# Global keys folded into the next-tile score blocks, and the first batch reordered, in a fused attention and phase-mixing kernel

## The chip, the cores and the metric

The kernel runs on one core of a Trainium2 chip. The metric is the device time of one execution in microseconds (us). A "median" is the median of several executions; the "span" is the length of one profiled execution from its first to its last instruction and is about 2 us shorter than its time. Engines are named as in the profile: PE is TensorE (PEld its weight loads), DVE is VectorE, ACT is ScalarE, POOL is GpSimd, SP is SyncE; "PEclk" is the TensorE clock that was granted, as a share of full speed.

## The reference

There are two stages. The first is attention with 4 batches, 8 heads, 768 positions and 64 columns per head. A query sees the keys 0 to 95 positions behind it and the first 8 keys ("global" keys), whatever their distance:

```python
rel = pos[:, None] - pos[None, :]
is_global = pos[None, :] < 8
is_local = (rel >= 0) & (rel < 96)
dist = np.where(is_global & ~is_local, 96.0, np.abs(rel))
scores = scale * q @ k.T - slope[h] * dist       # where is_global | is_local, else -1e9
x = softmax(scores) @ v                          # heads side by side: (4, 768, 512)
```

The second stage takes x, per batch:

```python
theta = x @ w_theta                              # (768, 512)
y = w_tok_r @ (x * cos(theta)) + w_tok_i @ (x * sin(theta))
u = x + y
out = u + relu(u @ w_ch)
```

## The kernel before

A sequence is 6 tiles of 128. Scores are built transposed, keys on the partitions. A tile of 128 keys is seen by 224 queries: its own 128, and the first 96 of the next tile. The exponentials are multiplied with a table `etab` that holds the exponential of the distance bias, and zeros where nothing is to be seen. Two heads form a pair; a 64-row matmul of each runs in one half of the array.

```python
def globals_(b):                                   # the 8 global keys, all queries, once per batch
    for hh in range(2):
        pg = ps_big()...
        for p in range(NP):                        # 4 pairs, 32 rows of the output each
            for c0, c1 in ((0, 512), (512, S)):
                nc.tensor.matmul(pg[GS*p:GS*(p+1), c0:c1], lhsT=kT[R, 0:GS], rhs=qT[R, c0:c1], ...)
        nc.scalar.activation(e_, pg[:, 0:S], AF.Exp, scale=scale, bias=gbias[:, hh:hh+1])
        nc.vector.tensor_mul(e_[:, 0:T], e_[:, 0:T], gmask)

def scores(b, p, c):                               # two key tiles: 2 tiles x 2 heads, 224 columns
    for j in range(2):
        jt = 2 * c + j
        n = min(W, S - jt * T)                     # W = 224
        for hh in range(2):
            nc.tensor.matmul(pb[:, hh, j*W:j*W+n], lhsT=kT[R, jt*T:(jt+1)*T], rhs=qT[R, jt*T:jt*T+n], ...)
    ...                                            # exp on ACT, times etab on DVE

def vglob(b, p):                                   # v of the global keys to the pair's 32 rows
    nc.tensor.matmul(pv, lhsT=shift[:, p, :], rhs=vn[:, 2*p:2*p+2, 0, :], ...)
    nc.scalar.copy(out=vg, in_=pv)

def values(b, p, hh):                              # 17 matmuls: own tile, tile before, globals
    for it in range(NT):
        mms = [(e_t[:, hh, it, 0:T], vn[:, 2*p+hh, it, :])]
        if it:
            mms.append((e_t[:, hh, it-1, T:2*T], vn[:, 2*p+hh, it-1, :]))
        mms.append((egs[b][hh][:, it*T:(it+1)*T], vg[:, hh, :]))
        ...
```

The second stage is PE work: `theta` (x times w_theta), `mix` (the two 768 x 768 token matrices) and `chan` (u times w_ch). The attention of batch b+1 is woven between the matmuls of `mix` of batch b. Batch 0's attention has nothing to hide behind; it is a prologue in which the order on PE is fixed by hand. `theta` needs x transposed and `chan` needs u transposed. For batches 1 to 3 both are DMAs, and `chan` of a tile comes two tiles behind its `mix`:

```python
def utrans(b, tt):
    if b and (b, tt) != (B - 1, NT - 1):
        nc.sync.dma_start_transpose(out=uT, in_=u)     # SP's queue
        return
    ...                                                # else on PE, copied by ACT

def chan(b, tt):
    for dc in range(NC):
        nc.tensor.matmul(ps_c, lhsT=uT[:, dc, :], rhs=w_ch_bf[:, dc, :], ...)
```

q, k and v are loaded with a change of type by DMAs from POOL. The tile for a batch's q and k has one buffer, so the load of the next batch's q and k starts when the last pair of this one has been copied out of it.

The softmax here doesn't subtract the row's maximum and nothing guards it: scores larger than these inputs give would overflow.

## Time and profile before

The median was 193.61 us (193.41 to 193.78, 3 runs). The profiled execution took 192.08 us (span 190.0 us, clock 1.00) and is quicker than those three.

The page of the kernel before, its parts 1 (busy time and share of each engine), 2 (clock in 40 slices, in tenths) and 4 (the chain of work that ended last, by engine):

```profile
PE 174.4 (92%) x1616; PEld 89.8 (47%) x1641; DVE 131.3 (69%) x305; ACT 108.0 (57%) x162; POOL 27.0 (14%) x31
PEclk9999999999999999999999999999999999999999
PE 65%; ACT 15%; DVE 8%; DMA 6%; issue 3%; POOL 1%; ACTq 0%; SPq 0%; POOLq 0%
```

PE is the engine to relieve, but not everywhere.

What the pieces cost on PE stands in the chain of waits, in order of time (start, length, what), taken from the mix of batch 1:

```profile
91.90 0.45 PE pb L227 x8
92.34 0.32 PE ps L352
...
93.65 0.30 PE pb L249 x4
93.95 0.54 PE ps L352 x2
94.48 0.52 PE pb L298 x17
...
97.26 0.97 PE ps L377 x4
```

L227 is half of the global scores, L249 a chunk of local scores, L298 the values of a head, L352 mix and L377 chan. A mix matmul takes 0.216 us among its like, but 0.32 us before a group of 64-row matmuls. The Trainium skill (TensorEngine Tiling (Array Packing), Key Properties) says that a change of tiling mode drains TensorE; the extra 0.1 us here agrees.

### The profile page before, as it was taken

To read this page: it belongs to the slowest core of one execution; us is meant where nothing else is said; L and a number is where in the kernel's file an instruction comes from. 1 tells how busy PE (TensorE), PEld (TensorE's weight loads), DVE (VectorE), ACT (ScalarE), POOL (GpSimd) and SP (SyncE) were. 2 spreads that over 40 slices of the span, in tenths; PEclk is the share of its full clock that TensorE was granted. 3 is DMA by queue.
4 is the path that set the end of the run, shared out by engine and by line. 5 is a ranking of instruction groups with operands and counts; after the bars stand their busy time and mean duration, and the time that the engine had idled before them with its cause. 6 is when DMAs were issued, how large, how long until landed. Compare 5 with 4: busy or idle time off the path is not lost.

```text
span 190.0 us, 3965 instructions
## 1 busy us (share of the span) xinstructions
PE 174.4 (92%) x1616; PEld 89.8 (47%) x1641; DVE 131.3 (69%) x305; ACT 108.0 (57%) x162; POOL 27.0 (14%) x31
## 2 busy tenths in 40 slices
PE   7868698999999999999999999999999999999981
PEld 2434386445735565643354454543554454434430
DVE  4699696487976886996587568986667753734422
ACT  2399987842697764489963450899644704800010
POOL 7992264000030002130000000000000000000000
PEclk9999999999999999999999999999999999999999
DMA  4999999999999833999925458111145254114432
GB/s 61 162 173 158 209 210 208 204 197 146 128 182 219 124 97 100 113 161 192 207 45 120 122 123 131 56 55 31 24 104 124 54 139 141 59 29 109 138 86 110
DMA packets 58082, 23.98 MB, mean 126 GB/s; under 512 B 44240, under 2 KB 54992, under 8 KB 58064
## 3 DMA queue, kind: packets, MB, share of 16 engines
q0 software_dynamic: 35760, 12.85, 72.2%
q1 hardware_dynamic: 22304, 10.88, 23.1%
q8 instruction: 13, 0.21, 0.4%
q14 instruction: 5, 0.04, 0.1%
HBM read 25.69 MB, written 6.29 MB: 168 GB/s over the span
## 4 chain that ended last, share of the span: by engine, by line
PE 65%; ACT 15%; DVE 8%; DMA 6%; issue 3%; POOL 1%; ACTq 0%; SPq 0%; POOLq 0%
PE ps L352 27%; PE ps L377 10%; PE pb L333 9%; PE pb L298 7%; PE pb L249 5%; DMA uT<-u 3%; PE ps L207 3%; DMA qk<-in_k_dram 3%; ACT cs L337 2%; ACT kT L214 2%; ACT e_108 L253 2%; PE ps L170 2%; DVE qT L212 1%; DVE qkn L199 1%; DVE zri L341 1%
## 5 line engine op out<-in xcount | busy, mean ns | idle before, releaser
L352 PE MATMUL ps<-zri,w_tokT_119 128*128 128x512 bf16 x136 | 51.6, 381 | 1.2 <-DVE zri L341 0.5
L352 PE MATMUL ps<-zri,w_tokT_120 128*128 128x512 bf16 x138 | 52.2, 379 | 0.5 <-issue 0.2
L377 PE MATMUL ps<-w_ch_bf,uT 128*128 128x512 bf16 x89 | 23.5, 380 | 1.2 <-DMA uT<-u 0.6
L341 DVE TENSOR_TENSOR zri<-x_sb,cs 128x512 bf16<-128x512 bf16 x48 | 18.3, 422 | 9.1 <-ACT cs L337 7.7
L357 DVE TENSOR_TENSOR u<-x_sb,ps 128x512 bf16<-128x512 bf16 x24 | 16.5, 686 | 11.6 <-PE ps L352 11.1
L333 PE MATMUL pb<-w_theta_bf,xT 128*128 128x512 bf16 x93 | 23.2, 379 | 0.2
L352 PEld LDWEIGHTS <-w_tokT_119 128*128 128x128 bf16 x144 | 14.0, 97 | 17.8 <-issue 4.2
L380 DVE SCALAR_TENSOR_TENSOR o_sb<-ps,u 128x512 f32<-128x512 f32 x24 | 16.5, 686 | 7.5 <-PE ps L377 6.6
L214 ACT COPY kT<-ps 128x768 bf16<-128x768 bf16 x16 | 12.9, 806 | 12.9 <-PE ps L207 12.8
L352 PEld LDWEIGHTS <-w_tokT_120 128*128 128x128 bf16 x144 | 14.1, 98 | 12.5 <-issue 1.4
L371 ACT COPY uT<-ps 128x512 bf16<-128x512 bf16 x7 | 4.1, 587 | 27.0 <-PE ps L370 27.0
L249 PE MATMUL pb<-qT,kT 64*128 64x224 bf16 x192 | 17.2, 254 | 2.3 <-ACT e_110 L253 0.7
L337 ACT ACTIVATE cs<-pb,halfpi 128x1024 bf16<-128x1024 f32 x12 | 13.4, 1119 | 9.1 <-issue 7.2
L207 PE MATMUL ps<-ident,qkn 128*128 128x128 bf16 x192 | 15.0, 222 | 0.9 <-DVE ident L101 0.4
L207 PEld LDWEIGHTS <-qkn 128*128 128x128 bf16 x192 | 11.9, 99 | 7.8 <-DVE qkn L199 5.5
L212 DVE COPY qT<-ps 128x768 bf16<-128x768 bf16 x16 | 15.1, 948 | 0.0
L249 PEld LDWEIGHTS <-kT 64*128 64x128 bf16 x192 | 6.3, 94 | 16.1 <-issue 13.5
L78 POOL DMA_DIRECT2D vn<-in_v_dram x5 | 9.5, 1921 | 24.9 <-DVE rec L306 20.9
L333 PEld LDWEIGHTS <-xT 128*128 128x128 bf16 x96 | 8.9, 98 | 8.8 <-ACT xT L319 0.3
L377 PEld LDWEIGHTS <-uT 128*128 128x128 bf16 x96 | 8.1, 98 | 10.4 <-DMA uT<-u 2.1
L199 DVE COPY qkn<-qk 128x768 bf16<-128x768 bf16 x30 | 10.8, 387 | 3.1 <-DMA qk<-in_q_dram 3.1
L177 PE MATMUL ps<-zero 128*128 128x512 bf16 x28 | 10.4, 473 | 2.4 <-DVE zero L88 1.4
(129 smaller groups left out, 280.9 us busy)
## 6 DMA issues: line engine op xcount, KB each, us to landing
out_dram<-o_sb SPq DMA_DIRECT2D x24, 256.0 KB, 2.3
qk<-in_q_dram POOLq DMA_DIRECT2D x3, 768.0 KB, 8.6
qk<-in_k_dram POOLq DMA_DIRECT2D x3, 768.0 KB, 12.3
vn<-in_v_dram POOLq DMA_DIRECT2D x3, 768.0 KB, 23.5
w_nat<-in_moe_w_tok_r_dram POOLq DMA_DIRECT2D x3, 384.0 KB, 15.9
w_nat<-in_moe_w_tok_i_dram POOLq DMA_DIRECT2D x3, 384.0 KB, 16.8
qk<-in_q_dram POOLq DMA_DIRECT2D x4, 192.0 KB, 5.3
qk<-in_k_dram POOLq DMA_DIRECT2D x4, 192.0 KB, 5.8
```

What stands on the lines that cost most here:

```text
L207: nc.tensor.transpose(ps[:, t_, :], qkn[:, t_, i_].rearrange("p h d -> p (h d)"), ident)
L212: nc.vector.tensor_copy(out=dst, in_=src)
L214: nc.scalar.copy(out=dst, in_=src)
L249: nc.tensor.matmul(pb[:, hh, j * W:j * W + n], lhsT=kT[R, jt * T:(jt + 1) * T], rhs=qT[R, jt * T:jt * T + n], start=True, stop=True)
L298: nc.tensor.matmul(o, lhsT=l_, rhs=r_, start=(i_ == 0), stop=(i_ == len(mms) - 1))
L333: nc.tensor.matmul(pb[:, j, :], lhsT=xT[:, dc, st * T:(st + 1) * T], rhs=w_theta_bf[:, dc, :], start=(dc == 0), stop=(dc == NC - 1))
L337: nc.scalar.activation(cs[:, 0], pb, AF.Sin, bias=halfpi)
L341: nc.vector.tensor_mul(zri[b][:, i_, 2 * c + j_, :].rearrange("p (g d) -> p g d", g=NP), xb[:, :, 2 * c + j_, :], cs[:, i_, j_].rearrange( ...
L352: anchor["pe"] = nc.tensor.matmul(ps, lhsT=w_tokT[wi][:, st, tt * T:(tt + 1) * T], rhs=zri[b][:, wi, st, :], start=(st == 0 and wi == 0), ...
L357: anchor["dve"] = nc.vector.tensor_add(u_sb[b, tt].rearrange("p (g d) -> p g d", g=NP), x_sb[b][:, :, tt, :], ps.rearrange("p (g d) -> p g ...
L377: nc.tensor.matmul(ps_c, lhsT=uT[:, dc, :], rhs=w_ch_bf[:, dc, :], start=(dc == 0), stop=(dc == NC - 1))
L380: nc.vector.scalar_tensor_tensor(o_sb, in0=ps_c, scalar=0.0, in1=u, op0=ALU.max, op1=ALU.add)
```

## The change

In the second score block of a key tile (the next tile's 128 queries), only keys 33 to 127 are ever near enough: the first rows of that block are always zero. The change puts the 8 global keys into rows 0 to 7 of these blocks. For that it makes a copy `kG` of the transposed keys, and a copy `vG` of v, in which the first 8 keys of each tile are replaced by the global ones. All blocks become 128 wide, the table gets five slots of 128 (the own block of the first tile, where the global keys are seen by every later query; a next-tile block; the own block of other tiles; and the last two again, so that each chunk finds its slots in a row), and the global scores, their exponentials, the shift matmuls and 6 of the 17 value matmuls per head go away. The first batch's order is also rewritten: v is loaded before the last two pairs of q and k, and values and x transposes are interleaved with the scores instead of coming at the end.

```diff
     alloc_loads(0)
-    for p in range(NP):
-        load_qk(0, 2 * p, 2)
+    load_qk(0, 0, 2)
+    load_qk(0, 2, 2)
     load_v(0, 0, 4)
+    load_qk(0, 4, 2)
+    load_qk(0, 6, 2)
     load_v(0, 4, 4)
 ...
+        nc.vector.tensor_copy(out=kG, in_=kT[:, T:(NT - 1) * T].rearrange("p (t n) -> p t n", t=NT - 2))
+        nc.vector.tensor_copy(out=kG[:, :, 0:NG], in_=kT[:, None, 0:NG].to_broadcast([T, NT - 2, NG]))
 ...
-    def globals_(b):
-        ...
     def scores(b, p, c):
 ...
-            n = min(W, S - jt * T)
-            for hh in range(2):
-                nc.tensor.matmul(pb[:, hh, j * W:j * W + n], lhsT=kT[R, jt * T:(jt + 1) * T],
-                                 rhs=qT[R, jt * T:jt * T + n], start=True, stop=True)
+            for part in range(2 if jt + 1 < NT else 1):
+                for hh in range(2):
+                    lhsT = kG[R, jt - 1, :] if part and jt else kT[R, own]
+                    o = (2 * j + part) * T
+                    nc.tensor.matmul(pb[:, hh, o:o + T], lhsT=lhsT, rhs=qT[R, (own, nxt)[part]],
+                                     start=True, stop=True)
 ...
+    def vglob(b, h0, n):
+        with behind("dve"):
+            nc.vector.tensor_copy(out=vG[:, hs], in_=vn[:, hs, 1:NT - 1, :])
+        nc.vector.tensor_copy(out=vG[0:NG, hs], in_=vn[0:NG, hs, 0:1, :].to_broadcast([NG, n, NT - 2, D + 1]))
     def values(b, p, hh):
 ...
-                mms.append((e_t[:, hh, it - 1, T:2 * T], vn[:, 2 * p + hh, it - 1, :]))
-            mms.append((egs[b][hh][:, it * T:(it + 1) * T], vg[:, hh, :]))
+                mms.append((e_t[:, hh, it - 1, 1, :], vG[:, h, it - 2, :] if it > 1 else vn[:, h, 0, :]))
 ...                                              # the prologue of batch 0
-        for p in range(1, NP):
-            prep(0, p, 2 if p == 1 else 0)
-            ...
-            for c in range(NT // 2):
-                scores(0, p - 1, c)
-                warm(1)
-        globals_(0)
-        ...                                       # last pair's scores, all values, all x transposes
+        for p in range(1, NP + 1):
+            if p < NP:
+                prep(0, p, 2 if p == 1 else 0)
+                bias_table(p)
+            if p == 2:
+                vglob(0, 0, 4)
+            if p == 3:
+                vglob(0, 4, 4)
+            for c in range(NT // 2):
+                scores(0, p - 1, c)
+                if p == 1:
+                    warm(1)
+            if p > 1:
+                values(0, p - 2, 0)
+                values(0, p - 2, 1)
+            if p > 2:
+                xtrans(0, p - 3, nc.scalar.copy)
```

`warm(n)` is n matmuls on zeros that nothing reads; they keep PE's clock up. `behind("dve")` places a copy in the order behind the last u addition.

## The prediction

> **What bounds the kernel now.** TensorE. The page has PE busy 174.4 of 190.0 us, DVE 69%, ACT 57%; PE holds 65% of the chain that ended last; the granted clock is 1.00. By stretches: from 35.7 to 152 us PE is busy 98%. The first 35.7 us differ: from 9.5 to 23.5 us ACT is busy 14.00 of 14.00 us, PE only 10.0; the chain there runs DMA, then ACT. The last stage (165 to 190 us) has no attention. At the batch boundaries (76 to 84.3, 116 to 126 us) DVE is also full: 8.30 of 8.30 and 9.70 of 10.0.
>
> **What goes from PE, per batch** (chain and timeline views):
> - global scores: 2 groups of 8 matmuls, 0.45 us each, plus about 0.095 us each because the matmul before them takes 0.31 instead of 0.216 us: 1.1 us. The Trainium skill (TensorEngine Tiling, Key Properties) says a change of tiling mode drains the array; these gaps agree.
> - 4 shift matmuls, 0.113 us start to start: 0.45 us.
> - values: 11 matmuls instead of 17 per head; 17 take 0.52 us, so 48 x 30 ns = 1.45 us.
>
> **Added to PE:** 22 score matmuls of 128 columns per head pair instead of 12 of 224/128. The two row halves overlap: a 224 pair takes about 107 ns, a chunk 298 ns with the drain. A 128 pair should take 56 to 67 ns, a chunk about 340: about 0.1 us per head pair, 0.4 us per batch. If weight loads hold pairs to 107 ns, it is +0.45 us per head pair.
> Net about -2.55 us per batch; three batches' attention lies in the PE-bound stretch: -7.6 us.
>
> **Other engines.** ACT loses, per batch, two global exponentials (0.95 us) and four vg copies (0.28), and gains about 0.08 us per head pair; eight table exponentials grow from 0.39 to about 0.52 us. DVE gains kG copies (about 0.35 us per head pair, scaled from 0.34 us for 768 elements) and vG copies (about 1.2 us per batch at the four-element rate that the skill, VectorE: DVE Perf Modes, gives for bf16 copies in SBUF; the qkn copies agree), and loses 0.45 us of gmask work: about +2 us per batch.
>
> **What is given back.** The kG copies fall into the boundaries where DVE is full: +0.3 us each. Without the globals, the first pair's values follow its scores sooner (about 1.8 instead of 3.8 us): +0.3 us per batch. Together +1.8.
> Prologue: no globals, values interleaved; but v is loaded before the third pair, and DVE, in order, waits for v at the vG copies (landings estimated at 11.6 and 19.2 us); ACT work hardly shrinks: only -0.7 us.
>
> **Prediction:** 193.6 - 7.6 + 1.8 - 0.7 = 187.1 us, range 183.8 to 190.0. Faster 0.82, same 0.16, slower 0.02.
>
> **What would show it.** Value groups of 11 matmuls in about 0.34 us; score chunks 0.33 to 0.36 us start to start (0.47 means weight-load bound); both mix stretches (89 to 116, 126 to 152 us before) 2 to 2.5 us shorter; first theta within 1.5 us of before; last stage equal; ACT down about 10 us, DVE up about 5.
>
> **What would make it wrong.** vG copies at one element per cycle[...]; score pairs bound by weight loads; the two score buffers shared with values making PE wait for exponentials that less PE work covers; a prologue that waits for v lengthen, or that gains several us because values no longer queue at its end.

## More of the kernel before

The windows view gives busy time per engine in stretches. I cut the span at six milestones: the first sine of batch 0; the last u of batch 0; the first and last u of batch 1; the first and last u of batch 2. The stretches are then the prologue, the mix of batch 0, a boundary (theta, and preparing the next q and k), the mix of batch 1, a boundary, the mix of batch 2, and the rest. The columns are: stretch, its length, busy time and count for PE, PEld, DVE, ACT and POOL, granted clock, DMA share, GB/s.

```profile
0.00:34.08 34.08, 27.17 (x326) 15.69 (x329) 24.64 (x84) 24.97 (x45) 21.26 (x26) 1.00 1.38 169
34.08:75.89 41.81, 40.05 (x427) 22.86 (x434) 32.47 (x71) 27.09 (x40) 2.98 (x3) 1.00 1.77 155
75.89:90.12 14.23, 13.86 (x104) 7.12 (x104) 12.16 (x28) 10.95 (x13) 2.73 (x3) 1.00 1.42 154
90.12:116.17 26.05, 25.74 (x268) 12.52 (x272) 17.61 (x36) 14.09 (x24) 0.00 (x0) 1.00 0.63 116
129.82:155.98 26.16, 25.60 (x267) 12.39 (x270) 17.60 (x36) 14.09 (x24) 0.00 (x0) 1.00 0.34 81
```

In the three mix stretches PE is busy 96 to 99% of the time; in the prologue only 80% (27.17 of 34.08). A matmul removed from a mix stretch should shorten it; one removed from the prologue need not.

## The result, and the profile after

| | before | after |
|---|---|---|
| median, us | 193.51 (193.34 to 193.78, 4 runs) | 191.17 (190.57 to 191.51, 4 runs) |
| profiled execution, us | 192.08 | 191.4 |
| span, us | 190.0 | 189.6 |
| granted clock, mean | 1.00 | 0.973 |

The ratio is 0.9874, with a 95% interval of 0.9844 to 0.9905. A ratio here is the mean time of one kernel's fast runs over that of the other's fast runs of the same rounds, so it is not quite the ratio of the medians. The kernel is 1.3% faster, which at a threshold of 2% counts as the same, and the time is above the predicted range.

The page of the kernel after, the same three parts:

```profile
PE 167.9 (89%) x1500; PEld 89.1 (47%) x1523; DVE 137.9 (73%) x309; ACT 102.9 (54%) x122; POOL 27.1 (14%) x31
PEclk9999669999999999999987999999999999999999
PE 55%; ACT 14%; DVE 13%; DMA 12%; issue 2%; POOL 2%; ACTq 0%; POOLq 0%
```

PE is 6.5 us less busy, yet the span is only 0.4 us shorter. DMA has gone from 6% to 12% of the chain, and the clock has two dents, in the slices from 19 to 28 us and from 95 to 104 us. The windows view of the kernel after, cut at the same milestones:

```profile
0.00:35.49 35.49, 26.36 (x293) 16.84 (x296) 25.96 (x76) 24.82 (x35) 21.03 (x26) 0.90 1.29 175
35.49:75.38 39.89, 37.91 (x399) 21.87 (x405) 34.10 (x74) 25.51 (x30) 4.14 (x3) 1.00 1.84 146
75.38:89.33 13.95, 13.79 (x111) 7.22 (x112) 13.00 (x36) 10.88 (x13) 1.88 (x3) 1.00 1.37 144
89.33:117.83 28.50, 24.88 (x233) 12.16 (x236) 18.66 (x32) 12.45 (x14) 0.00 (x0) 0.94 0.66 124
131.51:155.64 24.13, 23.06 (x232) 11.66 (x234) 18.58 (x32) 12.45 (x14) 0.00 (x0) 1.00 0.44 86
```

Some matmul records are missing from each trace, so the counts of PE are a few per cent off. The lengths are not affected. As differences, after less before (from the milestones before they were rounded for the view, so that a last digit can differ):

| stretch | before | after | difference |
|---|---|---|---|
| prologue | 34.08 | 35.49 | +1.41 |
| mix of batch 0 | 41.81 | 39.89 | -1.92 |
| boundary | 14.23 | 13.95 | -0.28 |
| mix of batch 1 | 26.05 | 28.50 | +2.45 |
| boundary | 13.65 | 13.69 | +0.04 |
| mix of batch 2 | 26.16 | 24.12 | -2.04 |
| rest | 33.98 | 33.99 | +0.01 |

Two of the three mix stretches gained 2 us each, as intended. The mix of batch 1 does the same work as that of batch 2, took almost the same time in the kernel before, and now takes 4.38 us longer. The prologue is 1.4 us longer. These are the two questions.

**The mix of batch 1.** The chain of the kernel after, from its start:

```profile
90.08 8.61 DMA uT<-u
98.69 0.05 issue
98.74 1.89 PE ps L357 x4
...
102.49 0.33 PE pb L278 x11
102.83 0.33 PE pb L230 x8
```

L357 is chan, L278 the values of a head and L230 a score chunk. The last two lines are the intended gain: 0.33 us instead of 0.52 for values, 0.33 instead of 0.30 for a chunk. The lines above are new. The transpose of batch 1's first u tile took 8.61 us, and PE waited for it. Its four matmuls then took 1.89 us instead of 0.97, at a lowered clock (0.50 for 3.41 us, from 98.45 us on). The summary line of the transposes of u (issue to landing), for the kernel before:

```profile
DMA to landing us min/median/max: 2.4/2.4/6.0
```

and for the kernel after:

```profile
DMA to landing us min/median/max: 2.4/2.4/8.6
```

The longest is the first of batch 1 in both. Before, it was issued at 90.9 and landed at 96.9, and chan wanted it at 97.26: 0.4 us to spare, invisible in the profile. At the same time the q and k of batch 3 are being loaded. The DMA view between 80 and 100 us gives the times from issue to landing, before:

```profile
qk<-in_k_dram POOLq DMA_DIRECT2D x1, 768.0 KB, 12.3
```

and after:

```profile
qk<-in_k_dram POOLq DMA_DIRECT2D x1, 768.0 KB, 13.6
```

With the issue at 84.02 and 84.85 us (timeline of POOL), k landed at 96.3 and 98.4 us, and the transpose within 0.6 us of it in both. So the sum closes: PE was ready for chan 1.4 us sooner (its last matmul before the wait ended at 95.84, where chan began at 97.26 before), the transpose landed 1.8 us later (98.7 against 96.9), and 0.4 us were to spare; that gives the wait of 2.9 us. The Trainium skill (DMA: Bandwidth & Descriptors, Queues, rings and completion order) says that each DMA engine takes turns between queues at packet granularity, so a short transfer shares with a long one. No run here shows the turns, and sharing need not be all of it. A store of the output stands ahead of the transpose on SP's queue. In the kernel after it was issued at 86.04 us and took 7.2 us (DMA view between 80 and 100 us); in after_qk2, below, the store before the same transpose took 2.0 us:

```profile
out_dram<-o_sb SPq DMA_DIRECT2D x1, 256.0 KB, 7.2
```

It landed at 93.26 us, and the packet records of the trace have the transpose's first 256-byte packet at 93.94 us, 3.9 us after its issue (93.19 and 94.04 us in the kernel before; in after_qk2 the first packet follows the issue by 1.2 us). So the load may have delayed the transpose in part by way of the store. No run moved the store, so the shares are open.

**The prologue.** The windows view of the kernel before, in the busy part:

```profile
14.00:19.00 5.00, 4.24 (x48) 2.37 (x47) 5.00 (x13) 5.00 (x11) 1.38 (x2) 1.00 2.78 158
19.00:24.00 5.00, 3.32 (x52) 1.78 (x51) 2.87 (x7) 5.00 (x12) 1.28 (x2) 1.00 1.19 209
```

and of the kernel after:

```profile
14.00:19.00 5.00, 2.90 (x46) 2.08 (x48) 5.00 (x16) 4.59 (x7) 2.38 (x4) 1.00 1.86 183
19.00:24.00 5.00, 4.03 (x64) 3.36 (x64) 5.00 (x16) 4.80 (x8) 2.18 (x3) 0.59 1.17 209
```

Before, ACT had no gap from 9.5 us to 24 us. After, DVE is full from 14 to 24 us (5.00 of 5.00 twice), ACT is not, and in the second window PE runs at a clock of 0.59. The timeline (start, length, engine, line, what, and in brackets the idle time before it and what ended it) shows the start of it in the kernel after:

```profile
12.38 0.43 DVE L259 COPY vG<-vn 128x1040 bf16<-128x1040 bf16 x1 [3.48 <-DMA vn<-in_v_dram]
...
14.41 2.64 ACT L234 ACTIVATE e<-pb 128x1024 bf16<-128x1024 f32 x3 [1.75 <-PE pb L230]
```

where the kernel before had

```profile
12.59 1.71 ACT L253 ACTIVATE e_108<-pb 128x896 bf16<-128x896 f32 x2
```

DVE, which works in order, waited 3.48 us for v, and behind the copy of v stood the copies that the second pair's scores and the kG of the first needed. The first exponential came 1.8 us later.

One caution for all prologues below. Traces of one and the same prologue differ: the first sine came at 34.08 and 34.99 us in the kernel before and in before_qk2, and at 35.49, 35.94 and 36.49 us in the kernel after, after_qk2 and after_uTpe. So the new prologue is 0.5 to 2.4 us longer by these traces, and a difference of less than 1 us between two single traces shows nothing.

### The profile page after: what moved, and what is told of

The parts are those of the page before. It is cut to its first block, busy times and chain, and to the rows that moved or that the text cites. A ratio compares the mean times of both kernels' runs of the same rounds, so it can differ in the third digit from the quotient of the medians.

```text
span 189.6 us, 3693 instructions
## 1 busy us (share of the span) xinstructions
PE 167.9 (89%) x1500; PEld 89.1 (47%) x1523; DVE 137.9 (73%) x309; ACT 102.9 (54%) x122; POOL 27.1 (14%) x31
## 4 chain that ended last, share of the span: by engine, by line
PE 55%; ACT 14%; DVE 13%; DMA 12%; issue 2%; POOL 2%; ACTq 0%; POOLq 0%
PE ps L332 22%; PE ps L357 10%; DMA uT<-u 8%; PE pb L313 7%; ACT e L234 6%; PE pb L230 5%; DMA vn<-in_v_dram 4%; PE pb L278 4%; DVE qT L203 4%; ACT cs L317 3%; PE ps L198 3%; DVE qkn L189 2%; PE ps L278 2%; DVE zri L321 2%; POOL qk L72 2%
## 5 line engine op out<-in xcount | busy, mean ns | idle before, releaser
L234 ACT ACTIVATE e<-pb 128x1024 bf16<-128x1024 f32 (+1 forms) x48 | 44.1, 958 | 25.8 <-PE pb L230 25.7
L357 PE MATMUL ps<-w_ch_bf,uT 128*128 128x512 bf16 x94 | 25.3, 391 | 3.7 <-DMA uT<-u 3.5
L242 DVE TENSOR_TENSOR e<-e,etab 128x1024 bf16<-128x1024 bf16 (+1 forms) x32 | 19.7, 617 | 3.5 <-ACT e L234 3.5
L230 PE MATMUL pb<-qT,kT 64*128 64x128 bf16 x224 | 17.9, 231 | 4.7 <-ACT e L234 4.6
L230 PEld LDWEIGHTS <-kT 64*128 64x128 bf16 x224 | 10.0, 99 | 18.3 <-issue 16.7
L278 PEld LDWEIGHTS <-e 128*128 128x128 bf16 x352 | 14.7, 100 | 6.8 <-issue 1.0
L198 PE MATMUL ps<-ident,qkn 128*128 128x128 bf16 x192 | 16.1, 232 | 1.1 <-DVE qkn L189 0.9
L198 PEld LDWEIGHTS <-qkn 128*128 128x128 bf16 x192 | 12.8, 103 | 8.4 <-DVE qkn L189 6.1
L230 PE MATMUL pb<-qT,kG 64*128 64x128 bf16 x128 | 13.6, 228 | 2.0 <-DVE kG L210 2.0
L357 PEld LDWEIGHTS <-uT 128*128 128x128 bf16 x96 | 8.4, 99 | 13.5 <-DMA uT<-u 4.7
```

The lines of the kernel that those rows point to most:

```text
L198: nc.tensor.transpose(ps[:, t_, :], qkn[:, t_, i_].rearrange("p h d -> p (h d)"), ident)
L230: nc.tensor.matmul(pb[:, hh, o:o + T], lhsT=lhsT, rhs=qT[R, (own, nxt)[part]], start=True, stop=True)
L234: ins = nc.scalar.activation(e_c, pb[:, :, 0:n], AF.Exp, scale=scale).ins
L242: nc.vector.tensor_mul(e_c, e_c, tab[:, :, s0:s0 + n // T].rearrange("p a s n -> p a (s n)"))
L278: nc.tensor.matmul(o, lhsT=l_, rhs=r_, start=(i_ == 0), stop=(i_ == len(mms) - 1))
```

## The experiments

All kernels gave correct results. Kernels of one group ran on one chip and share the runs of the kernel before. Each edit is against the kernel after unless it says otherwise.

### Group 1: the two causes, one at a time

Theory: the lost time of batch 1 is the DMA transpose slowed by the load of q and k, and the prologue's is DVE's wait for v. Rivals: the stretch of batch 1 is slow because the new attention work itself stalls PE there; and the prologue is slow because of the cold clock.

**after_qk2** takes the load away from the transpose. With two q and k buffers it can start much earlier. To fit in memory, other buffers had to shrink; PE, ACT and DVE keep their order of work.

```diff
-        qk = ld.tile([T, 2, H, NT, D], BF, name="qk", bufs=1)
+        qk = ld.tile([T, 2, H, NT, D], BF, name="qk", bufs=2)
...                       # qT, kT, kG: bufs 6 -> 4; vG: bufs 2 -> 1
```

> The changed kernel with two buffers for the q and k loads in place of one (fewer buffers of qT, kT, kG and vG make room); the order of the compute instructions is the same, only the loads of later batches move earlier. Theory A (TensorE's saving in batch 1's mix was lost because the first two DMA transposes of u there share the DMA engines with the q/k load of batch 3, and TensorE now arrives before they land): the first transpose lands in about 2.4 us in place of 8.6, the 3 us wait near 98 us goes, the clock stays at 1.00 there, the stretch between the first and the last u of batch 1 takes about 25 us in place of 28.5, the whole kernel about 188 us. Rival B (the score buffers and the exponentials limit that stretch): the stretch stays at 28 us, the kernel at 191.

Median 187.39 us (186.91 to 188.62, 4 runs) beside 193.33 us of the kernel before (7 runs, 191.99 to 195.7, two of them slow), ratio 0.9723 (0.9655 to 0.9792). The summary line of its transposes of u, and, from its windows view, the mix of batch 1:

```profile
DMA to landing us min/median/max: 2.4/2.4/3.8
```

```profile
89.78:113.90 24.12, 23.61 (x237) 11.86 (x236) 18.58 (x31) 12.46 (x14) 0.00 (x0) 1.00 0.41 93
```

The first transpose of batch 1 took 2.45 us, the stretch took 24.12 us instead of 28.50, exactly that of batch 2, and the clock was 1.00. No other stretch moved by more than 0.5 us (prologue 35.94, first mix 39.89, boundaries 13.95 and 13.69, last mix 24.12). PE's attention work there was never the trouble.

**after_uTpe** leaves the loads alone and takes the transpose off the DMA: this one tile of u is transposed on PE and copied by ACT.

```diff
-        if b and (b, tt) != (B - 1, NT - 1):
+        if b and (b, tt) not in ((1, 0), (B - 1, NT - 1)):
             nc.sync.dma_start_transpose(out=uT, in_=u)
```

> The changed kernel with only the first u tile of batch 1 transposed by TensorE and ScalarE in place of a DMA. Theory A: the wait of 2.9 us for this one transpose goes, at 0.3 us of added TensorE work, so 2.5 to 3 us less: about 188.5 us. Rival B: no change, 191.

Median 188.04 us (186.9 to 188.91), ratio 0.9744 (0.9666 to 0.9822). The mix of batch 1 took 24.69 us:

```profile
90.32:115.01 24.69, 23.75 (x241) 12.18 (x241) 18.67 (x31) 12.95 (x15) 0.00 (x0) 1.00 0.67 138
```

The DMA share, 0.67, is that of the kernel after (0.66), so the load was still there. The stretch pays 0.57 us for the transposes on PE and is 3.8 us shorter all the same. Both ways of parting the two transfers remove the loss, so its cause is shown: the transpose meeting the load. By which path (shared DMA engines, or the slowed store ahead in SP's queue) is not shown.

**after_vglate** moves the vG copies of batch 0 behind the first multiplication of the next pair's scores, so that DVE does not stop for v.

```diff
-        with behind("dve"):
+        with behind("dve" if b else "mul"):      # "mul": the table multiplication of the chunk just before
...
-            if p == 2:
-                vglob(0, 0, 4)
-            if p == 3:
-                vglob(0, 4, 4)
             for c in range(NT // 2):
                 scores(0, p - 1, c)
+                if p in (2, 3) and c == 0:
+                    vglob(0, 4 * (p - 2), 4)
```

> The changed kernel with batch 0's vG copies placed behind the table multiply of the next pair's first scores on VectorE, so that VectorE does not wait for the v load ahead of the first kG and qT. Theory C (that 3.5 us wait of VectorE delays the first exponential from 12.6 to 14.4 us and with it the whole prologue by 1.4): first exponential near 12.8 us or before, first theta 1 to 1.5 us sooner, the kernel 1 to 1.5 us faster. Rival D (the prologue is longer because ScalarE's exponentials are as many and TensorE runs at half clock from 19 to 28 us): first exponential sooner, but first theta moves by less than 0.5 us.

Median 195.42 us (194.51 to 196.63), ratio 1.0134 (1.0059 to 1.0209): slower than either kernel. The wait for v was gone and the first exponential came at 13.09 us instead of 14.41, but the first sine came at 39.22 us instead of 35.49. Later lines of ACT's timeline of this kernel:

```profile
18.61 2.64 ACT L234 ACTIVATE e<-pb 128x1024 bf16<-128x1024 f32 x3 [1.57 <-PE pb L230]
...
25.44 0.80 ACT L205 COPY kT<-ps 128x768 bf16<-128x768 bf16 x1 [3.37 <-PE ps L198]
```

DVE now stood at the copies of the third and fourth pairs' q and k, in order as before, and waited for each load (the chain goes through the k of the fourth pair, which landed at 17.24 us). Removing the one wait uncovered the next. My theory of the prologue, one wait for v, was too small.

**after_warm** has warming matmuls after every chunk of all pairs, as the kernel before had for its first three.

```diff
-                if p == 1:
-                    warm(1)
+                warm(1)
```

> The changed kernel with one filler matmul after every score chunk of the prologue, as the kernel before has it (the change kept it for the first pair alone). Theory D: the clock in the slices from 19 to 28 us goes from about 0.6 back to 1.0, values and transposes there halve, first theta about 1 us sooner. Theory C: the clock may rise, but first theta moves by less than 0.4 us, because ScalarE and VectorE set the pace.

Two of its four runs fell in the slow state, the profiled one among them, so its median (190.5 us; 187.85 to 191.92) and its ratio (0.9792, 0.9667 to 0.9917) are unclear. In the profile the clock is 1.00 from 19 to 29 us, and the first sine still comes at 35.27 us, 0.2 us sooner than in the kernel after. That speaks against the cold clock as the prologue's whole cause, but does not settle it: this execution had the half clock from 14.7 to 18.1 us instead, and the two fast runs (187.85 and 189.94 us) left no trace.

### Group 2: a control, and the prologue's order

**before_qk2** is the kernel before with two q and k buffers and nothing else. If the kernel before also lost time to the meeting, it should gain.

> The kernel before, with two buffers for q and k loads and nothing else. Theory A says that the first u transposes of batch 1 land late in both kernels, and that the kernel before mostly hid it because TensorE came to them later (in its profile the first took 6.0 us and nothing waited 2 us): then it gains at most 1.5 us, to about 192, much less than the 3.5 us that the changed kernel gained. If it gains as much, the transposes held both kernels alike and are no reason for the lost saving.

Median 193.5 us (192.96 to 194.17, 6 runs), ratio 0.9978 (0.9936 to 1.002), beside 194.11 us of the kernel before (11 runs, 192.17 to 194.83). The mix of batch 1 took 26.05 us, as before. So two buffers are worth nothing by themselves; they are worth 4.4 us of that stretch only since the change made PE arrive 1.4 us sooner and the load start 0.8 us later.

**after_qkfirst** only loads all of q and k before v, as the kernel before did.

```diff
-    load_qk(0, 0, 2)
-    load_qk(0, 2, 2)
+    for p in range(NP):
+        load_qk(0, 2 * p, 2)
     load_v(0, 0, 4)
-    load_qk(0, 4, 2)
-    load_qk(0, 6, 2)
     load_v(0, 4, 4)
```

> The changed kernel with the load order of the kernel before (all q and k of batch 0, then v). VectorE still runs the program's order, which now has four qkn copies ahead of the first kG: first exponential about 14.6 us as in the changed kernel, but the later waits for loads are shorter. Theory E (the prologue is set by what VectorE's fixed order makes wait for a load, whichever it is): first theta moves by -0.5 to -1.5 us against the changed kernel. If the load order itself were the whole cause: -1.5 us or more and first exponential at 12.6.

Median 193.32 us (192.78 to 194.47), ratio 0.9983 (0.9938 to 1.0029): slower than after. DVE now waited for the copies' loads first and then for v (1.44 us, v landing after 16 us); the first exponential came at 15.36 us and the first sine at 36.91 us. The mix of batch 1 was longer too, 29.95 us.

**after_order** is after_qkfirst, with the vG copies moved as in after_vglate, and the third and fourth pairs' copies held behind the kG copies of the pair before. DVE then meets its work in the order in which its data arrives.

```diff
-        with behind("dve"):
+        with behind("dve" if b else "kG"):       # "kG": the second kG copy of the pair before
...                                               # and the edits of after_qkfirst and after_vglate
```

> As after_qkfirst, with two moves in VectorE's order: qkn copies of the third and fourth pair behind kG of the pair before, and the vG copies behind the next pair's first table multiply. Now nothing on VectorE waits for a load ahead of kG and qT. Theory E: first exponential about 12.7 us, no wait of ScalarE above 1 us after it, first theta 2 to 3.5 us sooner than in the changed kernel, whole about 188. Rival F (the prologue is bound by ScalarE's sum of work, which did not shrink): first theta at most 1 us sooner.

Median 190.91 us (189.47 to 193.76), ratio 0.9814 (0.9761 to 0.9868). Two of six runs, the profiled one among them, were slow, so I read the order from the next kernel. It is **after_order_qk2**, which adds the two buffers.

> after_order with the two q/k buffers of after_qk2. The two causes lie in different stages, so the gains should add: about 184.5 us, that is 4.5% under the kernel before. If the earlier prologue only runs into the next load, less than 1 us under after_qk2.

Median 188.72 us (188.06 to 189.65), ratio 0.9733 (0.9691 to 0.9775), so the gains did not add to 184.5 us. The first exponential came at 11.90 us, earlier than in either kernel, and still the first sine at 36.32 us. A line of its ACT timeline, and a line of its windows view:

```profile
21.30 0.80 ACT L203 COPY kT<-ps 128x768 bf16<-128x768 bf16 x1 [2.32 <-PE ps L196]
```

```profile
19.00:24.00 5.00, 4.15 (x61) 3.60 (x59) 4.22 (x11) 2.70 (x4) 1.94 (x3) 0.50 1.17 207
```

The prologue's start was mended and its middle was not. In PE's hand-made order the fourth pair's q and k are transposed after the first pair's values, and those wait for the vG copies. At a clock of 0.50 the values' last 18 matmuls then took 1.15 us and the 12 transposes 1.29 us (chain of waits); ACT had nothing to do for 2.32 us.

### Group 3: what lies in the middle of the prologue

All four build on after_order_qk2. Theory: the interleaved order and the cold clock together cost the time. Rival: the folded work itself (kG and vG copies, wider exponentials) makes the prologue longer in any order.

**after_order_warm** warms with three matmuls after each chunk of the later pairs.

```diff
-                if p == 1:
-                    warm(1)
+                warm(1 if p == 1 else 3)
```

> after_order_qk2 with three filler matmuls after every score chunk from the second pair on. In after_order_qk2 the first exponential came at 11.9 us and still the first theta was late, with the clock at 0.5 from 19 to 29 us and ScalarE waiting 2.3 us for transposes. Theory G (with the late start gone, TensorE at half clock is what the prologue waits for): clock 1.0 there, first sine 1.5 to 2.5 us sooner than its 36.1 us, whole about 186.5 us. Rival H (the place of the values in TensorE's order, ahead of the next pair's transposes and behind vG, holds ScalarE whatever the clock): first sine within 0.7 us of 36.1.

The first sine came at 33.79 us, 2.5 us sooner and no later than in the kernel before, with a clock of 1.00 from 19 to 29 us (values' last 18 matmuls 0.70 us, the 12 transposes 0.67 us). But the time was 189.76 us (189.04 to 190.1, 4 runs), ratio 0.9815 (0.9776 to 0.9855), a smaller gain than without. The boundary before the mix of batch 1 had grown from 13.95 to 18.95 us:

```profile
73.69:92.64 18.95, 15.66 (x113) 8.48 (x112) 13.32 (x36) 11.08 (x13) 0.09 (x1) 0.91 0.96 117
```

Its waits between 72 and 84 us (engine, line, for what, us in total, times, longest):

```profile
PE pb L314 <- DMA xT<-x_sb: 3.3, 3, 2.6
```

theta of batch 1 waited 3.3 us in all, and after the longest wait 12 transposes took 1.21 us instead of 0.67 (mean clock of the boundary 0.91). The transposes of x took 8.7 us in the middle and 11.2 us at most in this kernel, where the kernel after has 3.3 and 6.3 us. With two buffers the load of batch 3 runs right there: the k that was issued at 53.70 us took 21.3 us to land. That load is the one that was taken away from the transposes of u. It is not the whole account: k landed at 74.96 us, but the transpose of the longest wait, issued at 72.20 us, only at 79.78 us, with a load of v under way (71.56 to 85.23 us). In order_warm_uTpe (group 4), with one buffer, the same transpose beside the same load of v took 2.8 us. So the second buffer brings the delay, but through which transfer is not shown.

**after_fill** puts the values and x transposes of earlier pairs before the third chunk of a pair, so that PE should have something to do. **after_fill_warm** adds three warming matmuls to it after each of the first two chunks (for the first pair after all three).

```diff
             for c in range(NT // 2):
+                if c == 2:
+                    if p > 1:
+                        values(0, p - 2, 0)
+                        values(0, p - 2, 1)
+                    if p > 2:
+                        xtrans(0, p - 3, nc.scalar.copy)
                 scores(0, p - 1, c)
...                                               # and not after the chunks
```

> after_order_qk2 with the values of pair p-2 moved, on TensorE, from behind the third score chunk of pair p-1 to ahead of it, where TensorE waits for a score buffer anyway. Theory H: ScalarE's wait of 2.3 us for the fourth pair's transposes falls below 1 us, first sine 1.5 us or more sooner than 36.1 us even without filler matmuls. Theory G: less than 0.7 us sooner, since the clock stays low.

> Both: values ahead of the third chunk, and three filler matmuls after the first and second chunks. If G and H each hold a part, first sine at about 32.5 us, 3.5 us sooner than in after_order_qk2, and the whole about 185 us; this would be the fastest kernel. If the prologue is then bound by the sum of ScalarE's work (about 13.5 us of copies and exponentials from the first one on), not below 31.5 us.

Both missed what they were made for. The first sine came at 36.14 and 36.72 us: now the third chunk waited behind values (ACT idle for 2.17 us before it in after_fill). The times were 187.54 us (187.11 to 187.76), ratio 0.9698 (0.9656 to 0.9739), and 186.92 us (185.82 to 187.83), ratio 0.9671 (0.9611 to 0.973). These are better than after_order_warm, although their prologues are longer by over 2 us, because their boundary stayed at 13.95 us.

**after_valend** gives the folded kernel the prologue order of the kernel before: all scores first, one warming matmul per chunk, values and x transposes at the end.

> after_order_qk2 with the order of the kernel before on TensorE in the prologue: score chunks of all pairs with one filler matmul each, values and x transposes only at the end; so here the change is the folding of the global keys alone. If interleaving the values is what costs in the changed prologue: first sine at or before the 34.1 us of the kernel before and the exponentials without waits above 1 us; the tail after the last exponential grows to 7 us. If the folding itself (kG, vG and table copies on VectorE) is what costs: first sine stays above 35 us.

ACT's timeline of this kernel:

```profile
19.92 5.45 ACT L234 ACTIVATE e<-pb 128x1024 bf16<-128x1024 f32 x6
...
33.51 1.11 ACT L318 ACTIVATE cs<-pb,halfpi 128x1024 bf16<-128x1024 f32 x1 [0.65 <-PE pb L314]
```

Six exponentials stand without a gap where the interleaved order had waits, and the first sine comes at 33.51 us (34.09 us in valend_uTpe, with the same prologue), no later than in the kernel before. So the rival falls: with the loads and DVE in the repaired order, folding by itself does not lengthen the prologue. Median 187.79 us (187.27 to 189.65; the profiled execution is the slowest of the four), ratio 0.9735 (0.9674 to 0.9797), again with a longer boundary (18.55 us) and waits for the transposes of x.

### Group 4: settling why the repairs did not add

What was still open was whether the two longer boundaries came from the two buffers meeting an earlier prologue, or from the prologue order itself. Both kernels below go back to one q and k buffer (and the other buffers as they were), and take the transpose off the DMA as after_uTpe does. **order_warm_uTpe** has the prologue of after_order_warm, **valend_uTpe** that of after_valend.

> The same with after_order_warm's prologue (values between the pairs, three filler matmuls). As above: 185 to 186.5 us if only the held transposes ate it, else 187.5 to 188.

> after_valend with one q/k buffer again and the first u tile of batch 1 transposed by TensorE. If loads that hold transposes are the only thing that ate the earlier prologue: the jump at the boundary to batch 1 (4.6 us between last u of batch 0 and first sine of batch 1 in the changed kernel, 9.3 in after_valend) is back at about 4.7 us, no wait of TensorE on a DMA above 1 us, whole 185 to 186 us, under after_uTpe's 188.0. If some other floor holds batch 1: 187.5 to 188, as after_uTpe.

| | median, us | ratio | first sine | boundary | mix of batch 1 |
|---|---|---|---|---|---|
| order_warm_uTpe | 186.05 (185.08 to 186.46, 6 runs) | 0.9613 (0.9572 to 0.9653) | 33.25 | 13.94 | 24.70 |
| valend_uTpe | 185.41 (184.62 to 186.18, 6 runs) | 0.9583 (0.9537 to 0.963) | 34.09 | 13.94 | 24.70 |

They ran beside 193.44 us of the kernel before (11 runs, 192.32 to 194.89). The windows view of valend_uTpe, boundary and mix of batch 1:

```profile
73.98:87.92 13.94, 13.86 (x112) 7.13 (x111) 12.99 (x35) 10.87 (x13) 1.88 (x3) 1.00 1.36 144
87.92:112.62 24.70, 23.76 (x241) 12.20 (x241) 18.66 (x31) 12.94 (x15) 0.00 (x0) 1.00 0.67 138
```

With one buffer the boundary is short again under both prologues, so it was the two buffers together with an early prologue. The gains now add, and valend_uTpe beats both kernels: 4.2% less than before. Its span of 183.94 us against 189.96 us is the stretches' sum: +0.02 in the prologue, -1.92, -0.29, -1.35, +0.04, -2.04 from the first mix to the last, and -0.47 in the rest.

## Why the prediction was wrong

The prediction was 187.1 us in a range of 183.8 to 190.0, and faster with a chance of 0.82. It was 191.17 us.

1. **The gain per batch was right.** "Net about -2.55 us per batch", less 0.6 us given back per batch, is about -1.95 us. Where no transfer stood in the way (after_qk2), the two later boundaries with their mix stretches took 75.88 us against 80.09 us in the kernel before, so -2.1 us per batch; the first mix gained 1.92 us. Value groups of 11 took 0.33 us ("about 0.34") and score chunks 0.33 us ("0.33 to 0.36"), so weight loads did not bind. The share given back was put in the wrong place: the boundaries were to grow by 0.3 us each and came out at -0.28 and +0.04, while the mix stretches gained 1.9 to 2.0 us and not 2.25 (2.55 less 0.3). The two misses offset each other, so that the sum came out this close is in part luck.

2. **The step that failed first is a missing one.** The sum took all three batches at their PE cost: "three batches' attention lies in the PE-bound stretch: -7.6 us". In its place the three mix stretches gave -1.92, +2.45 and -2.04 us, -1.5 us in all. The sum asked what PE must do and not what it would have to wait for once it was quicker. The transpose of the first u tile of batch 1 had 0.4 us to spare before, because it lands with the batch 3 load, which PE's work in that stretch does not hasten. PE came 1.4 us sooner, the transpose 1.8 us later, and PE waited 2.9 us; with the lowered clock after it the stretch took 4.38 us more than the same work in batch 2. Removing the meeting in two ways gave 24.12 and 24.69 us in place of 28.50. The hint was in the trace of before: a longest transpose of 6.0 us among a median of 2.4 us.

3. **The prologue went the other way.** "Only -0.7" was +1.41 us (0.5 to 2.4 us by all traces of the two prologues). The prediction had seen DVE wait for v ("DVE, in order, waits for v at the vG copies") and had the landing nearly right (11.6 us estimated, 12.36 us measured), but took it to be absorbed. It cost 1.8 us of the first exponential, and what followed was paced by a full DVE, by values standing before transposes in PE's order, and by a clock of 0.59. No one of them alone is the cause: moving the wait alone uncovered the waits for q and k (39.22 us), warming alone gave 0.2 us (in a slow run), ordering alone left the middle (36.32 us). Order and clock together gave 33.79 us; the old order on PE, with the loads and DVE repaired, gave 33.51 us. That the interleaving would make "values no longer queue at its end" and so could gain, which the prediction also considered, was the wrong hope: values interleaved in a fixed order delay the transposes behind them.

4. **Other sizes.** ACT lost 5.1 us, not "about 10": a pair's exponentials, counted from start to start, went from 2.28 to 2.52 us (+0.24, predicted 0.08), and the global exponentials and vg copies were taken at their full durations of 0.95 and 0.28 us though back to back they start every 0.80 and 0.16 us. DVE gained 6.6 us, not 5: the small kG copy takes 200 ns in the mean, together with the large one (285 ns) 0.49 us per pair ("about 0.35"). The vG copies cost 700 and 692 ns, so 1.4 us per batch ("about 1.2"); the Trainium skill (VectorE: DVE Perf Modes, Side-by-side: where the cycles go for N=2048 bf16) has 693 ns for a copy of 2048 at four elements per cycle, and 2080 elements here agree. ACT and DVE were not what decided the time in the mix stretches.

In spans the two failed steps are +2.1 us (prologue) and +4.4 us (the transpose). Together they are more than the miss of 4.1 us in the median, because the medians differ by 2.3 us and the two profiled spans by only 0.4 us: the profiled execution of the kernel before was quicker than its other executions. Where its usual executions spend the additional 1.4 us is not to be seen in its trace. The clock records give a lead: of its 34 fast runs in the four groups, the 13 with a mean clock of at least 0.995 (the profiled one had 1.00) have a median of 192.71 us, the 21 below it 193.85 us; and in before_qk2, whose prologue is the same, a half clock of 3.41 us from 22.86 us on went with a first sine 0.91 us later. No run tested it, so it stays open.

The 4.38 us can be split along the chain. From the first u of the batch to where PE was ready for chan both stretches took 6.51 us. Then came the wait of 2.90 us and, at the lowered clock, 0.92 us more for chan (1.89 us, in batch 2 0.97), 0.20 us for a score chunk (0.54, 0.34) and 0.36 us for four matmuls of mix (1.33, 0.97): 4.38 us together. No run had the wait without the lowered clock, so this is a sum and not a test.

## What to carry to other kernels

Before you count a saving on the busiest engine, list what that engine waits for just in time, and how much each of those transfers has to spare: a median latency of 2.4 us with a maximum of 6.0 us names a place where a quicker engine may have to stop, as here. Where engines work in a fixed order, removing one wait uncovers the next, so test repairs together and also look at the stages behind them: here two good repairs (an earlier load, a shorter prologue) met in a third place. When a change does two things, as here folding and a new prologue order, time them apart: folding with nearly the old order came to 0.9583 of the time before (valend_uTpe), with the new order to 0.9744 as it was written (after_uTpe) and to 0.9613 when that order was repaired and warmed as well (order_warm_uTpe). The intervals of 0.9583 and 0.9613 overlap, so the new order is not shown to be worse once repaired; it earned nothing.

## What the Trainium skill lacked or had wrong

- DMA: Bandwidth & Descriptors, and Advanced Engine Details and Errata (X-Bar Transpose (TRN2), "TRN2 transpose DMAs are as fast as regular DMAs"): neither gives a latency for a small transpose beside a large load on another queue. Here a 128 x 512 transpose took 2.4 us alone, 6.0 and 8.61 us beside a 768 KB load (and behind a store on its own queue that took 8.2 and 7.2 us), and a transpose of x 2.8 us alone and up to 11.2 us. The two of u landed within 0.6 us of the load; a transpose of x in after_order_warm landed 4.8 us after it.
- TensorE: Matmul & The Clock Gate (Part 1) speaks of an idle window of about 3.4 us before the clock falls to half. Here a wait of 2.90 us was enough for the four matmuls after it to take 1.89 instead of 0.97 us, and one of 2.60 us (after_order_warm, boundary) for the 12 transposes after it to take 1.21 instead of 0.67 us. In the first case PE had stood still for 2.61 us when the clock fell; in the second the clock fell 0.77 us after PE had begun again. Both times it stayed at half for 3.41 us. Warm and cold pitches agree with the page: 12 transposes of 128 columns took 0.67 us warm and 1.29 us cold, where its 55.6 and 106.7 ns give 0.67 and 1.28 us.
- TensorEngine Tiling (Array Packing), Key Properties, says that a mode switch drains TensorE but not what it costs: here the matmul before a group of 64-row matmuls took about 0.32 instead of 0.216 us.
